# Weight combinations of a two-layer transformer kernel, made by adding transfers from GpSimd

## The chip, the cores and the metric

The kernel runs on one core of a Trainium2 chip. The metric is the device time of one execution in microseconds (us), the median of several runs. The core's engines are TensorE (PE; weight loads are shown apart as PEld), VectorE (DVE), ScalarE (ACT), GpSimd (POOL) and SyncE (SP). Each works through a queue of its own in order; they wait for each other through semaphores. Transfers (DMAs) are issued by one of the queues and carried by 16 DMA engines.

## The reference

Two layers, each an attention part and a feed-forward part, on x of 2048 tokens by 1024:

```python
def A(x):                                   # H = 32 heads of 32, W = 8 keys, dilation 2
    q, k, v = split(x @ wqkv)
    logits[s, w] = q[s] . k[s - 2 w] * 32 ** -0.5      # masked where s - 2 w < 0
    return concat_heads(softmax(logits) @ v[s - 2 w]) @ wo
def B(x):                                   # F = 3584
    return relu(x @ w1 + b1) ** 2 @ w2 + b2
x = x + A(layernorm(x));  x = x + B(layernorm(x))
x = x + A(layernorm(x));  x = x + B(layernorm(x))
```

All inputs are bfloat16; the kernel works in float16 and bfloat16 with float32 sums.

## The kernel before

**Units.** A layer's tokens are cut into four groups of 512 (four tiles of 128). With two layers there are eight units, u = 0 to 7, and each goes through the same stages: `SA` (load x, LayerNorm, transpose into `xnA`), `SQ` or `SQ7` (q, k, v), `S2` (attention), `SW` or `SW7` (product with wo, residual, second LayerNorm into `xnB`), `SF1` (FFN1: relu squared, into `r2`) and `SF2` (FFN2, residual, `out_tile`). Unit u+1's attention is worked on while unit u's FFN runs.

**Seven products.** The large matrix products use a Strassen scheme in Winograd's form: a 2 by 2 block product from seven products (`product`, L657, order and banks from `seven` and `AT`) into PSUM banks X, Y and Z. Three of the seven take raw blocks of the weights (`RAW`), four take combinations of blocks (`COMB`: products 5, 7, 6, 3). The moving side has combinations too (`T`, `TA`, made by `rhs_combos`, L682). ACT copies the first product's bank to seed another (`seed_first`, L590), and DVE and ACT put the results together.

**Where the combinations are made.** The weights' combinations are the same for all units. They are made once, in units 0 and 1, by DVE: four tensor_tensor operations (`tv`) for each block, each followed by a store of 256 KB into DRAM scratch (`sw` for w1, `sqv` for q and v, `sk` for k; `tw` and `two` for w2 and wo). `keep_w1` (L661) does this for the seven blocks of w1 (28 operations, L674), `keep_wqkv` (L513) for k (8) and for q and v (16). Later units load them back by `w<-sw` and so on, 1 MB each. Unit 0 itself computes q, k, v without the scheme (`SQ`, chunks `pq` on PE at L879, cast by ACT at L884), and so does unit 1; unit 0's FFN1 (`SF1_plain`, L1196) does its first `PLAIN1` = 1 block of seven without it (`ph`, L1222 and L1226) and the others from the tiles that DVE has just made.

**Attention.** In `S2` (L920) DVE multiplies q with the shifted k (`P`, L941), sums the products of chunks in a tree (L949) of a given depth, and PE sums over the rest and over a head's lanes (`lg`, L956; four matmuls for each leaf). `DEP0` is that depth for the two halves of unit 0's tokens; eight chunks at depth 1 leave four leaves, at depth 3 one. After the softmax (ACT, DVE) DVE does the weighted sum with v (`pr`, `o`: L1020, L1027).

**The start.** Unit 0's tiles 0 to 2 of x are normalised by `ln_first` (statistics and normalisation on DVE), tile 3 by `ln` with statistics and normalisation on ACT (L740 to L750). PE transposes them (`pt`, L800), DVE copies the transposes to `xnA` (L803). `XACT` = (1, 2) puts the loads of two tiles on ACT's queue, the other loads are on SP's. Unit 1's LayerNorms follow on ACT (L740 to L748, L719).

**What sets the order.** The stages only register operations with an engine, an estimated duration, buffers and a priority. The class `Plan` simulates the engines with these durations, picks by priority, and shifts priorities by the lists of seeds in `ORDER`. What comes out is one fixed queue for each engine. At run time nothing but these queues and the waits for data and buffers sets the order; the argument `after` of an operation holds in the plan alone.

Of the kernel before, what the change touches and what calls it, by code (L numbers as in the profile page):

```python
# [27 lines left out]
FOLD = (0, 1, 2)  # L28
# [9 lines left out]
XACT = (1, 2)  # L38
# [10 lines left out]
DEP0 = (1, 1)  # L49
NEARLY = 4  # L50
PLAIN1 = 1
# [3 lines left out]
RT = 4  # L55
PR1 = 20.0
XT = 2
# [67 lines left out]
class Plan:  # L125
# [45 lines left out]
    def schedule(self):  # L171
# [19 lines left out]
        def fits(o):  # L191
            if o.mb and len(landed) >= LANES and landed[-LANES] > t + 1e-9:
# [28 lines left out]
        landed = []  # L221
# [3 lines left out]
        while left:  # L225
            progress = False
            for e in engs:
# [13 lines left out]
                if o.mb:  # L241
                    dma_free = max(dma_free, end) + o.mb / DMA_MBS
                    end = dma_free
                    landed.append(end + o.lat)
# [84 lines left out]
class _Kernel:  # L329
    def __init__(self, ctx, tc, x, wqkv, wo, w1, b1, w2, b2, out, n_layers=2):  # L330
# [16 lines left out]
        self.state = {}  # L347

    def setup(self):
# [36 lines left out]
        todo = {"k": [("k", 0), ("k", 1)], "qv": [("q", 0), ("q", 1), ("v", 0), ("v", 1)], "w1": list(range(self.NDP))}  # L386
        self.orders = {j: interleave(d) for j, d in todo.items()}
# [12 lines left out]
        p.caps.update(pk=2, pj=2, lg=4, w=8, xt=XT, P0=4, P1=4, pr=2, pb=2, dn=1, e=1, xm=6, xnA=1, xnB=1, xn=3, xo=2, q=1, k=1, v=1, o=1, r2=1, s1=1, tv=4, T=1, TA=1, tr=3, wl=2, u=6, y=4, yq=4, yxm=2, yxa=2, yxo=2, ri=1, yw=4, so=1)  # L400
# [12 lines left out]
    def dma(self, out, src, r, w, mb, prio=None, after=(), name="dma", cast=None, lat=None, eng="SP", dur=None):  # L413
# [3 lines left out]
        return self.p.add(eng, dur or 0.08, fn, r, w, self.nxt() if prio is None else prio, after, mb=mb, name=name, lat=lat)  # L417

# [140 lines left out]

    def seven(self, job, xnT, T, make):  # L560
# [6 lines left out]
        for d, pr in order:  # L567
# [8 lines left out]
            else:  # L576
                if d not in ws:
                    w = ws[d] = Buf("8K", "w", [128, 4, 4, 256], F16)
                    key = (job,) + (d if isinstance(d, tuple) else (d,))
                    self.dma(lambda w=w: w[:], lambda d=d: self.scr[job][d][:], [(key, i) for i in range(4)], [(w, 0)], 4 * 0.256, name="w")  # L580
# [5 lines left out]
    def seven_banks(self):  # L586
        return [Buf("ps", nm, [128, 2, HB], F32, "seeded" if nm == "Y" else "") for nm in "XYZ"]

    def seed_first(self, X, Y):
        self.p.add("ACT", act(512), lambda: self.nc.scalar.copy(Y[:], X[:]), [(X, 0)], [(Y, 0)], UP, name="u")  # L590

    def qkv_step(self, u, nm, s):
# [13 lines left out]
        def keep(i):  # L606
            us[i] = Buf("1K", "u", [128, 2, HB], F16)
            p.add("ACT", act(512), lambda: nc.scalar.copy(us[i][:], X[:]), [(X, 0)], [(us[i], 0)], UP, name="u")  # L608

        def copy(bank):  # L610
            y = Buf("1K", "yq", [128, 2, HB], F16)
            p.add("ACT", act(512), lambda: nc.scalar.copy(y[:], bank[:]), [(bank, 0)], [(y, 0)], 1.5, name="yq")  # L612
# [9 lines left out]
        def mul(pr, w, wi, rhs, rc):  # L622
            bank, fm = self.product(pr, w, wi, rhs, X, Y, Z)
            self.state[u]["gate" + nm] = p.add("PE", 8 * MMH, fm, rc + [(w, 0)], [(bank, 0)], self.nxt(), name="fq")
            if pr == 1:
                self.seed_first(X, Y)
            elif pr == 5:
                us["y5"] = copy(Z)
# [32 lines left out]
    def keep_w1(self, dp, w):  # L661

        nc, p = self.nc, self.p

# [12 lines left out]
        comb(s3, lambda: raw(0, 0), lambda: raw(1, 0), ALU.subtract, [(w, 0), (w, 1)], 7)  # L677
        comb(s2, lambda: s1[:], lambda: raw(0, 0), ALU.subtract, [(w, 0), (s1, 0)], 6)
        comb(s4, lambda: raw(0, 1), lambda: s2[:], ALU.subtract, [(w, 0), (s2, 0)], 3)
        return {5: s1, 7: s3, 6: s2, 3: s4}  # L680

    def rhs_combos(self, xnT, prio, cls, tag, whole=False):  # L682
# [9 lines left out]
        def comb(i, a, b, ra, tl):  # L692
            p.add("DVE", dve(512), lambda: nc.vector.tensor_tensor(t(i)[:, tl], a()[:, tl], b()[:, tl], ALU.subtract),
                  ra, [(T, (i, tl))], prio, name="T")
        if whole:
            def both(i, a, b, ra):
                p.add("DVE", dve(1024), lambda: nc.vector.tensor_tensor(t(i), a(), b(), ALU.subtract), ra, [(T, (i, 0)), (T, (i, 1))], prio, name="T")
            lo, hi = [(xnT, 0), (xnT, 1)], [(xnT, 2), (xnT, 3)]
            both(0, lambda: B(0, 1), lambda: B(0, 0), lo + hi)
            both(1, lambda: B(1, 1), lambda: t(0), hi + [(T, (0, 0)), (T, (0, 1))])  # L700
            both(2, lambda: B(1, 1), lambda: B(0, 1), hi)
            both(3, lambda: B(1, 0), lambda: t(1), lo + [(T, (1, 0)), (T, (1, 1))])
            return T
        for tl in range(2):
            lo, hi = [(xnT, tl)], [(xnT, 2 + tl)]
            comb(0, lambda: B(0, 1), lambda: B(0, 0), lo + hi, tl)
            comb(1, lambda: B(1, 1), lambda: t(0), hi + [(T, (0, tl))], tl)
            comb(2, lambda: B(1, 1), lambda: B(0, 1), hi, tl)
# [3 lines left out]
    def ln(self, x, xv, xcells, xnT, tl, prio, vec, on_pe=False, tag="xn", after=(), vnorm=True, pv=-99.5, parts=1):  # L712
# [48 lines left out]
        if on_pe:  # L761
            return self.transpose(xn, xnT, tl, -10.0 if pv == -99.5 else pv, parts), xn
# [30 lines left out]
    def transpose(self, xn, xnT, tl, prio, parts=1):  # L793
# [3 lines left out]
        for i in range(parts):  # L797
# [4 lines left out]
            def f6(i=i):  # L802
                nc.vector.tensor_copy(xnT[:, tl, i * n:(i + 1) * n], pt[:, i * n:(i + 1) * n])  # L803
            p.add("PE", 0.65 / parts, f5, [(xn, 0)], [(pt, i)], prio, name="pt")
            op = p.add("DVE", 0.09 + 0.6 / parts, f6, [(pt, i)], [(xnT, tl if i == parts - 1 else (tl, i))], prio - 200.0, name="ptc")
# [12 lines left out]
    def SA(self, u):  # L818
# [7 lines left out]
        for tl in ORD if u == 0 else range(4):  # L826
# [3 lines left out]
            if u == 0 and tl == 3:  # L830
                self.ln(x, xv, [0], xnT, tl, -9e4, False, on_pe=True, tag="xn3", after=rst)
# [364 lines left out]
    def SF1_plain(self, u):  # L1196
# [50 lines left out]
        for i, (dp, pr) in enumerate(interleave(range(PLAIN1, self.NDP))):  # L1247
# [4 lines left out]
            if pr in s:  # L1252
                step(pr, s[pr], None, *rhs[pr])
            else:
# [17 lines left out]
    def ffn1_step(self, r2, dp, fold):  # L1272
# [7 lines left out]
        def keep(i):  # L1280
            us[i] = Buf("1K", "u", [128, 2, HB], F16)
            if not fold:
                p.add("ACT", act(512), lambda: nc.scalar.copy(us[i][:], X[:]), [(X, 0)], [(us[i], 0), (us[i], 1)], UP, name="u")
                return
            f = f0 + (h if i == 3 else 0)
            for a in range(2):
                p.add("ACT", 0.1 + act(256), lambda a=a: nc.scalar.activation(out=us[i][:, a, :], in_=X[:, a, :], func=ACTF.Identity,  # L1287
                                                                              bias=self.b1T[:, f + a:f + a + 1], scale=1.0),
                      [(X, 0)], [(us[i], a)], UP, name="u")

        def copy(bank):
            y = Buf("1K", "y", [128, 2, HB], F16)
            p.add("ACT", act(512), lambda: nc.scalar.copy(y[:], bank[:]), [(bank, 0)], [(y, 0)], 1.5, name="y")  # L1293
# [30 lines left out]
        def mul(pr, w, wi, rhs, rc):  # L1324
            bank, fm = self.product(pr, w, wi, rhs, X, Y, Z)
            self.ffs.append(p.add("PE", 8 * MMH, fm, rc + [(w, wi[0] if isinstance(wi, tuple) else 0)], [(bank, 0)], self.nxt(), name="ff"))
            if pr == 1:
                self.seed_first(X, Y)
            elif pr == 2:
                relu(Y, r1, f0)  # L1330
            elif pr == 5:
                us["y5"] = copy(Z)
# [104 lines left out]
    def out_tile(self, layer, t, db, py, xm, end=False):  # L1437
# [5 lines left out]
        if not end:  # L1443
            xo = Buf("1K", "xo", [128, BLK], BF)
            self.merge(py, lambda: xm[:, sl], lambda: xo[:], [(xm, db)], [(xo, 0)], "xo")
            self.dma(lambda: dst[:, sl], lambda: xo[:], [(xo, 0)], [(cell, db)], 0.14, prio=-10.0)
            return
        for i in range(2):
            xo = Buf("1K", "xo", [128, HB], BF)
            a, c = slice(i * HB, (i + 1) * HB), slice(db * BLK + i * HB, db * BLK + (i + 1) * HB)  # L1450
            p.add("DVE", dve(HB, False), lambda xo=xo, a=a, c=c: nc.vector.tensor_tensor(xo[:], py[:, a], xm[:, c], ALU.add),
                  [(py, i), (xm, db)], [(xo, 0)], -100.0, name="xo")
            self.dma(lambda c=c: dst[:, c], lambda xo=xo: xo[:], [(xo, 0)], [(cell, (db, i))], 0.07, prio=-10.0)
# [34 lines left out]
    def build(self):  # L1488
# [8 lines left out]
        self.run(self.SQ(0, "v"))  # L1497
        self.biases()
# [46 lines left out]
def _lay(name, a):  # L1545
# [7 lines left out]
    if name == "A_wqkv":  # L1553
        a = a.reshape(2, 4, 128, 3, 128, 4, 2).transpose(3, 5, 2, 0, 1, 6, 4).reshape(3, 4, 128, 2, 1024)
        get = lambda d, m, k: a["qkv".index(d[0]), 2 * m + d[1], :, k]
        a = np.concatenate([a.reshape(-1)] + raws(get, [("k", 0), ("k", 1)]) + raws(get, [("q", 0), ("q", 1), ("v", 0), ("v", 1)]))
    elif name == "A_wo":
        a = a.reshape(128, 8, 2, 512).transpose(2, 0, 1, 3).reshape(256, 4096)
    elif name == "B_w1":
        a = a.reshape(8, 128, 2, 7, 256).transpose(3, 1, 2, 0, 4).reshape(7, 128, 2, 2, 1024)  # L1560
        a = np.concatenate([a.reshape(-1)] + raws(lambda d, m, k: a[d, :, m, k], range(7)))
# [27 lines left out]
```

## Time and profile before

| what | us |
|---|---|
| median of 3 runs (1133.49, 1133.62, 1139.12) | 1133.62 |
| profiled execution | 1134.86 |
| its span | 1133.1 |
| busy in the span: PE, DVE, ACT, POOL | 1122.6, 996.4, 800.2, 1.8 |
| first matmul of q and k (pq) starts at | 9.96 |
| last matmul ends at | 1129.74 |

The span is from the first to the last instruction of the profiled execution; 1.76 us lie outside of it. Busy times of engines overlap. In the rows of a profile, "128x512 f16" is partitions by elements and type, "xN" the number of instructions, and "<-" in brackets names what ended the idle time ahead of an instruction. The granted TensorE clock is 1.00 in all of the profile.

### The profile page before, as it was taken

The numbers are of one execution on the slowest core, as the hardware profiler recorded it, in microseconds if no ns is written. First come the engines' busy times: TensorE is split into PE (matmuls) and PEld (weight loads), VectorE is DVE, ScalarE is ACT, GpSimd is POOL, SyncE is SP. The second block draws the span as 40 slices with busy tenths as digits, with TensorE's granted clock in tenths as the row PEclk, the third lists the DMA queues.
The fourth block names the chain that finished last, engine by engine and source line by source line (L and its number), as shares of the span: only waits on it lengthen the run. The fifth ranks groups of instructions, "written<-read, shape, count | busy, mean of one in ns | idle before, by whom it ended". The sixth has DMA issues, their size and how long they took to land.

```text
span 1133.1 us, 20734 instructions
## 1 busy us (share of the span) xinstructions
PE 1122.6 (99%) x7872; PEld 771.8 (68%) x7919; DVE 996.4 (88%) x1541; ACT 800.2 (71%) x1602; POOL 1.8 (0%) x8
## 2 busy tenths in 40 slices
PE   8999999999999999999999999999999999999998
PEld 6645764678846787468864688557884678845864
DVE  7999999999997999959999699997999789997341
ACT  6733897467985789757993669856797478933861
POOL 0000000000000000000000000000000000000000
PEclk9999999999999999999999999999999999999999
DMA  9966789999999996999979997999979999689882
GB/s 368 289 207 242 233 265 322 324 350 366 379 348 365 350 387 251 337 357 362 369 264 359 381 335 278 333 313 416 347 268 331 374 378 377 215 314 311 333 301 93
DMA packets 141053, 362.34 MB, mean 320 GB/s; under 512 B 67866, under 2 KB 76186, under 8 KB 120602
## 3 DMA queue, kind: packets, MB, share of 16 engines
q1 hardware_dynamic: 140666, 360.50, 91.3%
q8 instruction: 62, 1.02, 0.4%
q10 hardware_dynamic: 288, 0.52, 0.1%
q14 instruction: 37, 0.30, 0.1%
HBM read 314.84 MB, written 31.46 MB: 306 GB/s over the span
## 4 chain that ended last, share of the span: by engine, by line
PE 90%; ACT 5%; DMA 3%; issue 1%; DVE 0%; DVEq 0%; SPq 0%; ACTq 0%
PE X L657 25%; PE X L1379 14%; PE Z L657 12%; PE Z L1379 7%; PE pq L879 7%; PE Y L657 6%; PE py L1075 4%; PE Y L1379 3%; PE py L479 3%; PE X L1146 3%; PE lg L956 1%; PE Z L1146 1%; ACT r L1314 1%; DMA w<-in_B_w_dram 1%; ACT u L1287 1%; ACT rr L1320 1%
## 5 line engine op out<-in xcount | busy, mean ns | idle before, releaser
L657 PEld LDWEIGHTS <-w 128*128 128x128 f16 (+1 forms) x4904 | 479.5, 98 | 72.2 <-DMA w<-in_B_w_dram 1.3
L1379 PEld LDWEIGHTS <-r 128*128 128x128 f16 x1183 | 115.7, 98 | 134.8 <-issue 0.2
L1379 PE MATMUL X<-w,r 128*128 128x512 f16 (+2 forms) x784 | 177.0, 377 | 0.4
L941 DVE TENSOR_TENSOR P<-q,k 128x2048 f16<-128x2048 f16 x128 | 153.9, 1225 | 1.9 <-ACT q L620 1.0
L657 PE MATMUL X<-T,w 128*128 128x256 f16 x1224 | 153.2, 273 | 0.0
L1020 DVE TENSOR_TENSOR pr<-pb,v 128x4096 f16<-128x4096 f16 x64 | 146.2, 2298 | 0.5 <-PE Y L657 0.3
L949 DVE TENSOR_TENSOR P<-P,P 128x2048 f16<-128x2048 f16 x106 | 129.2, 1222 | 0.2
L1314 ACT ACTIVATE r<-rr 128x1024 f16<-128x1024 f16 x110 | 123.9, 1140 | 0.5 <-DVE rr L1306 0.2
L1027 DVE TENSOR_TENSOR pr<-pr 128x1024 f16<-128x1024 f16 (+1 forms) x128 | 118.4, 955 | 0.0
L657 PE MATMUL X<-TA,w 128*128 128x256 f16 x864 | 108.6, 273 | 0.0
L590 ACT COPY Y<-X 128x512 f32<-128x512 f32 x115 | 70.6, 615 | 36.6 <-PE X L657 33.6
L879 PE MATMUL pq<-xnA,w 128*128 128x256 f16 (+1 forms) x512 | 86.5, 326 | 0.0
L1293 ACT CAST y<-Z 128x512 f16<-128x512 f32 x110 | 70.6, 655 | 6.0 <-PE Z L657 5.9
L879 PEld LDWEIGHTS <-w 128*128 128x128 bf16 x512 | 49.9, 98 | 32.1
L1297 DVE TENSOR_TENSOR rr<-u,y 128x512 f16<-128x512 f16 x110 | 46.2, 424 | 24.4 <-ACT y L1293 13.1
L1320 ACT ACTIVATE rr<-Y,b1T 128x256 f16<-128x256 f32 x110 | 54.2, 538 | 4.4 <-PE Y L657 3.3
L657 PE MATMUL Y<-xnB,w 128*128 128x256 f16 x440 | 56.7, 273 | 0.0
L657 PE MATMUL X<-xnB,w 128*128 128x256 f16 x440 | 55.9, 273 | 0.8 <-DMA w<-in_B_w_dram 0.8
L1320 ACT ACTIVATE rr<-X,b1T 128x256 f16<-128x256 f32 x110 | 55.7, 563 | 0.6 <-PE X L657 0.6
L612 ACT CAST yq<-Z 128x512 f16<-128x512 f32 x72 | 41.9, 586 | 18.5 <-PE Z L657 18.0
L608 ACT CAST u<-X 128x512 f16<-128x512 f32 x72 | 42.0, 586 | 18.2 <-PE X L657 17.5
L657 PE MATMUL Z<-xnB,w 128*128 128x256 f16 x392 | 50.8, 273 | 0.1
(159 smaller groups left out, 1648.8 us busy)
## 6 DMA issues: line engine op xcount, KB each, us to landing
w<-sw SPq DMA_DIRECT2D x49, 1024.0 KB, 10.3
w<-tw SPq DMA_DIRECT2D x56, 896.0 KB, 6.8
w<-in_B_w_dram SPq DMA_DIRECT2D x42, 896.0 KB, 5.8
w<-in_B_w_dram SPq DMA_DIRECT2D x35, 1024.0 KB, 10.9
w<-in_A_wqkv_dram SPq DMA_DIRECT2D x32, 1024.0 KB, 10.9
w<-sqv SPq DMA_DIRECT2D x24, 1024.0 KB, 11.2
w<-in_B_w_dram SPq DMA_DIRECT2D x28, 512.0 KB, 6.2
w<-sk SPq DMA_DIRECT2D x12, 1024.0 KB, 8.7
```

Of the source, the lines that this page charges most:

```text
L590: self.p.add("ACT", act(512), lambda: self.nc.scalar.copy(Y[:], X[:]), [(X, 0)], [(Y, 0)], UP, name="u")
L657: nc.tensor.matmul(bank[:, a, :], lw[:, k, a * 128:(a + 1) * 128], rhs(k), start=(start and k == 0 and a == 0), stop=(k == 3), skip_group_ ...
L879: nc.tensor.matmul(pq[:, t0 * HB:t1 * HB], w[:, c0 // 2 % 2, kd // 4, kd % 4, c0 % 2 * 128:c0 % 2 * 128 + 128], xnT[:, 2 * t0:2 * t1, kd, ...
L941: nc.vector.tensor_tensor(cur[:], q[:, c, None, hb * HB:(hb + 1) * HB].to_broadcast([128, W, HB]), _win_ap(k[:, c, :], HALO + hb * HB, HB) ...
L949: nc.vector.tensor_tensor(other[:], other[:], cur[:], ALU.add)
L1020: p.add("DVE", dve(4096), lambda pr=pr, ch=ch: nc.vector.tensor_tensor(pr[:], pb[:].unsqueeze(1).to_broadcast([128, 2, W, HB]), _win_ap2(v ...
L1027: nc.vector.tensor_tensor(dst, pr[:, :, 0:n, :], pr[:, :, n:2 * n, :], ALU.add)
L1293: p.add("ACT", act(512), lambda: nc.scalar.copy(y[:], bank[:]), [(bank, 0)], [(y, 0)], 1.5, name="y")
L1297: p.add("DVE", dve(512), lambda: nc.vector.tensor_tensor(r[:, :, m, :], us[i][:], y[:], ALU.add), [(us[i], 0), (us[i], 1), (y, 0)], [(r, ( ...
L1314: p.add("ACT", 0.955, lambda: nc.scalar.activation(out=r2[:, f:f + 2, :].rearrange("p a t -> p (a t)"), in_=r[:].rearrange("p a m t -> p ( ...
L1320: p.add("ACT", 0.36, lambda a=a: nc.scalar.activation(out=r[:, a, 0, :], in_=bank[:, a, :], func=ACTF.Relu, bias=self.b1T[:, f + a:f + a + ...
L1379: nc.tensor.matmul(banks[q][:, lo:hi], left(jj, q), w[:, j, lo:hi], start=(start and jj == 0), stop=(jj == h - 1), skip_group_check=True)
```

## The change

- **Combinations in DRAM.** For w1, q and v, `make` issues 44 transfers from GpSimd's queue: for each of eleven blocks (seven of w1, two each of q and v) a copy of 1 MB from DRAM to DRAM, bfloat16 to float16, and then transfers of 512, 256 and 256 KB that add to what lies there, each waiting for the one before it on that block. The host lays out copies of the weights' blocks for it (`SUM`). DVE's operations and stores for w1, q and v are gone; k's stay. `make` asks the planner to put the transfers after the last load of a weight for v.
- **All as sums.** An adding transfer can't subtract, so the combinations are sums, and the signs move to the combinations of the moving side, to ACT's copies (now activations of Identity with scale 1 or −1) and to the seed: product 1 goes to bank Y, and `seed_minus` writes X = −Y.
- **FFN1 of unit 0.** `PLAIN1` goes from 1 to 3; the other four blocks load their combinations from `sw` (1 MB each on SP's queue).
- **Logit tree of unit 0.** `DEP0` goes from (1, 1) to (3, 3).
- **The start.** Tiles 2 and 3 of unit 0 are normalised on ACT (`LNA`), and ACT copies their transposes (`CPT`). All four loads of x are on SP's queue.
- **Output.** `out_tile` writes the sum in place in `xm`, and rows are stored as tiles of 256 KB, not 128 KB each half (the last four tiles as before).
- **Order.** New seeds.

The matmuls on PE go from 2440 to 2480 of 128x512 and from 5414 to 5302 of 128x256; `tv` operations from 88 to 44; transfers on SP's queue from 600 to 534, on GpSimd's from 0 to 44.

```diff
-XACT = (1, 2)
+XACT = ()
...
-DEP0 = (1, 1)
+DEP0 = (3,3)
...
-PLAIN1 = 1
+PLAIN1 = 3
...
+SUM = ((1, 0), (0, 0), (0, 0), (0, 1), (1, 1), (1, 0))
+DM = ("w1", "qv")
+MKS = ("w1", "qv")
+LNA = (2, 3)
+CPT = ("xn3",)
...
+    def make(self, blocks, after=()):
+
+        p = self.p
+
+        def steps(job, d):
+            n = self.todo[job].index(d) + (2 if job == "qv" else 0)
+            src = (self.w1 if job == "w1" else self.wqkv)[self.at[job == "w1"] + n * 128 * 6144:][:128 * 6144].rearrange("(p n) -> p n", n=6144)
+            key = (job,) + (d if isinstance(d, tuple) else (d,))
+            dst = lambda a, b: self.scr[job][d][:, a:b].rearrange("p i k n -> p (i k n)")
+
+            def step(a, b, src, r, mb, op=None):
+                def fn():
+                    self.nc.gpsimd.dma_start(dst(a, b), src(), **({} if op is None else {"accum_op": op}))
+                return lambda: p.add("POOL", POOL_ISSUE, fn, r, [(key, i) for i in range(a, b)], self.nxt(), after, mb=mb, name="mk", lat=POOL_LAT)
+            return [step(0, 4, lambda: src[:, 0:4096], (), MK_COPY), step(0, 2, lambda: src[:, 4096:6144], (), 2 * MK_ADD, ALU.add),
+                    step(2, 3, lambda: dst(0, 1), [(key, 0)], MK_ADD, ALU.add), step(3, 4, lambda: dst(2, 3), [(key, 2)], MK_ADD, ALU.add)]
+
+        for i in range(0, len(blocks), 2):
+            for pair in zip(*[steps(*b) for b in blocks[i:i + 2]]):
+                for add in pair:
+                    add()
 
...
     def keep_wqkv(self, nm, ws, after=()):
...
+        if job in DM:
+            return
...
-            comb(s3, lambda: raw(0, 0), lambda: raw(1, 0), ALU.subtract, [w0, w1], 7)
-            comb(s2, lambda: s1[:], lambda: raw(0, 0), ALU.subtract, [w0, (s1, 0)], 6)
-            comb(s4, lambda: raw(0, 1), lambda: s2[:], ALU.subtract, [w0, (s2, 0)], 3)
+            comb(s3, lambda: raw(0, 0), lambda: raw(1, 0), ALU.add, [w0, w1], 7)
+            comb(s2, lambda: s1[:], lambda: raw(0, 0), ALU.add, [w0, (s1, 0)], 6)
+            comb(s4, lambda: raw(0, 1), lambda: s2[:], ALU.add, [w0, (s2, 0)], 3)
...
+    def combos(self, job, d):
+        w = Buf("8K", "w", [128, 4, 4, 256], F16)
+        key = (job,) + (d if isinstance(d, tuple) else (d,))
+        self.dma(lambda: w[:], lambda: self.scr[job][d][:], [(key, i) for i in range(4)], [(w, 0)], 4 * 0.256, name="w")
+        return w
...
+    def seed_minus(self, X, Y):
+        self.p.add("ACT", act(512), lambda: self.nc.scalar.activation(out=X[:], in_=Y[:], func=ACTF.Identity, scale=-1.0), [(Y, 0)], [(X, 0)], UP, name="u")
...
-        bank = {1: X, 6: X, 7: X, 4: X, 2: Y, 5: Z, 3: Z}[pr]
+        bank = {1: Y, 6: X, 7: X, 4: X, 2: Y, 5: Z, 3: Z}[pr]
...
     def keep_w1(self, dp, w):
+        if "w1" in DM:
+            return self.combos("w1", dp) if dp >= PLAIN1 else None
...
-            both(0, lambda: B(0, 1), lambda: B(0, 0), lo + hi)
+            both(0, lambda: B(0, 0), lambda: B(0, 1), lo + hi)
+            both(1, lambda: B(1, 1), lambda: t(0), hi + [(T, (0, 0)), (T, (0, 1))], ALU.add)
...
+        (nc.scalar.copy if act else nc.vector.tensor_copy)(xnT[:, tl, i * n:(i + 1) * n], pt[:, i * n:(i + 1) * n])
...
-            if u == 0 and tl == 3:
+            if u == 0 and tl in LNA:
+                self.ln(x, xv, [0], xnT, tl, -9e4, False, on_pe=True, tag="xn3", after=rst, vnorm=tl == 3)
...
         self.run(self.SQ(0, "v"))
+        ld = [o for o in self.p.ops if o.name == "w"][-1:]
+        self.make([(job, d) for job in MKS for d in self.todo[job]], ld)
         self.biases()
         self.S2(0, DEP0)
```

More of the change, by code (lines that the diff above doesn't have):

```diff
@@ L243, in schedule @@
                     end = dma_free
-                    landed.append(end + o.lat)
+                    landed[o.eng == "POOL"].append(end + o.lat)
                 out.append((t, len(out), o))
@@ L347, in __init__ @@
         self.state = {}
+        self.half = set()
     def setup(self):
@@ L1282, in keep @@
             if not fold:
-                p.add("ACT", act(512), lambda: nc.scalar.copy(us[i][:], X[:]), [(X, 0)], [(us[i], 0), (us[i], 1)], UP, name="u")
+                p.add("ACT", act(512), lambda: nc.scalar.activation(out=us[i][:], in_=X[:], func=ACTF.Identity, scale=-1.0 if i == 2 else 1.0), [(X, 0)], [(us[i], 0), (us[i], 1)], UP, name="u")
                 return
@@ L1331, in mul @@
             elif pr == 5:
[L1332 removed]
+                us["y5"] = copy(Z, -1.0)
             elif pr == 6:
@@ L1442, in out_tile @@
         cell = ("out" if final else "xs", layer, t)
[L1443 to L1446, printed above, removed]
-            return
[L1448 to L1453, printed above, removed]
+        o = lambda: xm[:].bitcast(BF)
+        if end:
+            for i in range(2):
+                a, c = slice(i * HB, (i + 1) * HB), slice(db * BLK + i * HB, db * BLK + (i + 1) * HB)
+                p.add("DVE", dve(HB, False), lambda a=a, c=c: nc.vector.tensor_tensor(o()[:, c], py[:, a], xm[:, c], ALU.add),
+                      [(py, i), (xm, db)], [(xm, (db, i))], -100.0, name="xo")
+                self.dma(lambda c=c: dst[:, c], lambda c=c: o()[:, c], [(xm, (db, i))], [(cell, (db, i))], 0.07, prio=-10.0)
+            return
+        self.merge(py, lambda: xm[:, sl], lambda: o()[:, sl], [(xm, db)], [(xm, db)], "xo")
+        if final and t >= self.NT - 4:
+            self.dma(lambda: dst[:, sl], lambda: o()[:, sl], [(xm, db)], [(cell, db)], 0.14, prio=-10.0)
+        elif t in self.half:
+            self.dma(lambda: dst, lambda: o(), [(xm, 0), (xm, 1)], [(cell, 0), (cell, 1)], 0.27, prio=-10.0)
+            self.half.discard(t)
+        else:
+            self.half.add(t)
     def run(self, a, b=(), pace=1):
```

85 lines of the change are left out of this document (47 added, 38 removed), and 16 rows, old and new, of the table ORDER.

## The prediction

> **What bounds the kernel now.** I read the engine rows of the page first, then the chain that ended last, then the windows.
>
> ```profile
> span 1133.1 us, 20734 instructions
> PE 1122.6 (99%) x7872; PEld 771.8 (68%) x7919; DVE 996.4 (88%) x1541; ACT 800.2 (71%) x1602; POOL 1.8 (0%) x8
> ...
> PE 90%; ACT 5%; DMA 3%; issue 1%; DVE 0%; DVEq 0%; SPq 0%; ACTq 0%
> ```
>
> TensorE is busy 99% of the span, at clock 1.00 throughout, and is the chain. So an edit pays by what it takes off PE's matmuls, and costs by any wait that it gives PE. POOL does next to nothing. The windows show where waits are near (busy us of each engine, clock, DMA share, GB/s):
>
> ```profile
> 5.00:10.00 5.00, 3.01 (x26) 1.63 (x25) 4.78 (x13) 2.92 (x8) 0.00 (x0) 1.00 1.03 409
> 10.00:30.00 20.00, 20.00 (x185) 17.26 (x184) 18.44 (x24) 15.81 (x43) 0.00 (x0) 1.00 1.03 406
> 60.00:90.00 30.00, 29.95 (x140) 13.51 (x140) 30.00 (x36) 11.30 (x20) 0.00 (x0) 1.00 0.47 161
> 90.00:110.00 20.00, 19.95 (x125) 10.78 (x125) 20.00 (x36) 8.31 (x20) 0.00 (x0) 1.00 0.88 320
> 110.00:170.00 60.00, 59.95 (x453) 44.08 (x452) 59.93 (x95) 52.84 (x105) 0.00 (x0) 1.00 0.76 243
> ```
>
> From 5 to 30 us the DMA engines are full at 406 to 409 GB/s; from 60 to 110 us VectorE (DVE) has no idle time and PE just none either. The order there decides, so I read the timeline: ACT at the start, DVE and PE where unit 0's FFN begins.
>
> ```profile
> 7.91 1.04 ACT L740 ACTIVATE xn<-x 128x1024 f16<-128x1024 bf16 x1
> ...
> 9.31 1.15 ACT L744 ACTIVATE xn<-x,sm 128x1024 f16<-128x1024 bf16 x1
> ...
> 11.04 0.38 ACT L884 CAST k<-pq 128x256 f16<-128x256 f32 x1
> ```
> ```profile
> 13.19 1.23 DVE L941 TENSOR_TENSOR P<-q,k 128x2048 f16<-128x2048 f16 x1 [0.23 <-ACT q L884]
> ...
> 111.58 0.69 DVE L803 COPY xnB<-pt 128x1024 f16<-128x1024 f16 x1
> ```
> ```profile
> 103.38 1.89 PE L879 MATMUL pq<-xnA,w 128*128 128x512 f16 x8
> ...
> 107.29 1.03 PE L1226 MATMUL ph<-xnB,w 128*128 128x256 f16 x8
> ```
>
> One LayerNorm on ACT delays the first cast by 3.1 us (7.91 to 11.04). DVE's run from the first product of unit 0's attention (13.19) to the last copy of FFN1's input (111.58, done 112.2) is one unbroken queue. PE does unit 1's chunks (pq) while it waits for that input, and starts FFN1 of unit 0 (ph) at 107.29.
>
> **The change, part by part.** Spacings on PE are 0.2157 us for a 512-wide matmul and 0.1091 for a 256-wide. From the first pq at 9.96 us, PE's matmuls times these spacings give 1115.6 us; the last one ends at 1129.74, so only 4.2 us were lost underway, and the tail is 3.4.
>
> *PE's work.* A tree at full depth saves 24 lg matmuls: −24 × 0.2157 = −5.2. Two more plain blocks add 64 ph of 512 (+13.8) and remove 112 of 256 from the products (−12.2). Together −3.6 us. The new sign pattern adds no matmul; ACT's copies become activations of the same shape (0.48 to the next one either way).
>
> *DVE's work up to FFN1 of unit 0.* I counted both queues between the two DVE lines shown. Before: 20 products and 10 tree sums at 1.135 from start to start, 22 combinations tv at 0.60, the eight av groups and the rest: 97.1 us; 13.2 + 97.1 = 110.3, against 112.2 in the trace, so the count holds within 2. After: products 26 (+6.8), tree sums 22 (+13.6), tv 8 (k's) instead of 22 (−8.4), two xnA copies gone to ACT (−1.2): 107.9. So DVE does fewer combinations in all (44 of 88 gone, some 26 us over the whole run), yet before FFN1 it has 10.8 us more: deeper trees, and unit 1's products moved ahead.
>
> *ACT at the start.* Tile 2's LayerNorm joins tile 3's on ACT, ahead of the first cast: 1.17 + 0.23 + 1.28 + 0.45 = 3.1 us, so the first cast goes to about 13.9. Up to the q cast that DVE's eighth product waits for, the queue then holds 16 casts (0.26), two LayerNorms of unit 1 (4.6 each: 1.17 + 0.23 + 1.28 + 0.8 + 1.14), one normalise (1.14), two small ones (0.5), and two copies of transposes, new on ACT (1.05 each, an estimate from the 128x512 cast's 0.585 and the 128x1024 activation's 1.14): 17.1, so it ends at 31. DVE's own queue would be there at 23.5 (13.2 + 10.3). DVE is 7.5 us late, and has no slack to 112. PE, whose banks wait for the same casts, loses about 4.6 by 29 us and 3.6 more at 60 to 64, inside what follows.
>
> *Where it lands.* 13.2 + 107.9 + 7.5 = 128.6 for the last xnB copy; ph can start about 1.2 earlier, 127.4. PE's own sum reaches that point at 113.85, because in the new order all 24 chunks of unit 1 stand ahead of it; before, 8 of them (13.8 us) were left to fill in. So PE waits 13.6 us in all. If that cover had stayed, this would cost nothing.
>
> *Inside FFN1 of unit 0*, without chunks between the products, ACT must free a bank for each product; it was busy 52.8 of 60 us at 110 to 170. Bounds 0 (it keeps up, as later) and 7 (the 88% over the 60 us that FFN1 takes, if it runs short by as much as it had idle). I take 3, nearer to the later units, where PE lost 4 us in 1000.
>
> *GpSimd's 44 transfers.* Eleven blocks, each a 1 MB copy from DRAM to DRAM and then adds of 512, 256 and 256 KB that wait for one another. No operation of this kind is in the trace. The first copies wait for no data (the "after" of the planner makes no wait), so 2 MB and the next steps fall into 5 to 30 us, where the engines are full. 1 MB at 410 GB/s is 2.44 us; between 0 MB and 4.2 MB land there. x of unit 1 has 2.5 us of slack before ACT needs it, the first weights have none: 0 to 9 us, I take 5, by the full share 1.03. The Trainium skill, DMA: Bandwidth & Descriptors, section Issuing engines are not separate DMA queues, says that GpSimd's transfers run on the same 16 engines and interleave; with half of 20 full microseconds it would be 10 here, and the sum 1157.
>
> *The chain of adds* after that: by the rows of before,
>
> ```profile
> w<-sw SPq DMA_DIRECT2D x49, 1024.0 KB, 10.3
> ...
> w<-in_B_w_dram SPq DMA_DIRECT2D x28, 512.0 KB, 6.2
> ...
> sqv<-tv SPq DMA_DIRECT2D x16, 256.0 KB, 5.6
> ```
>
> a pair of blocks takes 10.3 + 6.2 + 2 × 5.6 = 27.7 us, two at a time: the block that SP loads first (dp3) is ready at 55, dp6 at 103. SP gets to that load at about 100 us; PE wants the blocks from 149 to 165, plus its delay. Hidden, so 0, with a bound in the rival. The same four loads add 4 MB, in a window at share 0.76: 0. x loads all on SP: w is issued 0.85 us later, inside the 5 above. Stores of whole tiles from xm: off the path.
>
> *Sum.* 1134.9 (profiled execution) − 3.6 + 13.6 + 3 + 5 = 1152.9; the median of before lies 1.2 below its profiled run, so **1152 us**.
>
> **Rivals.**
>
> *GpSimd's chain holds SP's queue* (slower still). SP's load of dp3 waits for four adds, and raw weights of dp4, unit 2's x and its transposes are queued behind it. With every step f times as long, dp3 is ready at 55f and dp6 at 103f, landing 10.3 later, against about 183 for PE in the delayed schedule. It decides from f = 1.7; at f = 2 PE waits 33 us more (1185), at 2.5 it would be 85. For: an add must also read what it adds to, and DVE fills its time. Against: the rows used include queueing at a full share. The Trainium skill, SBUF — State Buffer, the warning on the "DVE blocks DMA" trap in the section SBUF: two separate sides, says that GpSimd cannot write descriptors while DVE holds the shared port; no row of before shows such a transfer.
>
> *The waits do not reach PE* (no change). If casts and LayerNorms on ACT overlap better than start to start, and DVE catches up as its tv work has gone, only −3.6 remains with part of the contention: 1128 to 1139, about 1131. For: DVE has 26 us less overall. Against: these 26 come mostly after FFN1 begins.
>
> *All waits vanish, the old ones too* (faster): −3.6 and up to the old 4.2: 1126. For: the old losses lie at 163 to 262 us, where DVE was full. Against: it needs chunks that no longer stand there to fill.
>
> *The change does not do what it says:* the transfers are meant for idle time (share 0.47 at 60 to 90) but start at launch. If all 4.2 MB get in ahead of first weights, 9 instead of 5, and 1156; this is in my own range.
>
> **How the numbers follow.** My case (1140 to 1163: contention 0 to 9, ACT 0 to 7) 0.60; the chain late (1163 to 1200) 0.21; waits not at PE (1128 to 1139) 0.12; all gone (below 1128) 0.07. Predicted 1152. The range of 1136 to 1184 leaves out the last case, some 0.07 of the third and 0.06 above. Half a per cent, 5.7 us, is about what a measurement of this kernel tells from no change: faster (below 1127.9) 0.07, same 0.12, slower (above 1139.3) 0.81.
>
> **What would show it.** Right: first cast on ACT near 14, DVE idle before a product near 24 to 31 with an ACT q cast as releaser; last xnB copy near 128; PE idle before ph and pt, released by DVE, together about 13 us from 20 to 130. After that PE's matmuls end 1008 + 3 to 7 us later. DMA share over 1 before 30 us with bytes on a POOL queue. Wrong: no PE idle before ph (the DVE count), waits on w<-sw with SP idle on POOL transfers (the chain), or first pq after 15 (contention heavier).

## The result, and the profile after

The changed kernel takes 1214.13 us (median of 3 runs, 1212.89 to 1214.22) against 1133.62: ratio 1.0697, interval 1.0676 to 1.0718. The forecast was 1152 with a range up to 1184. Slower was right; the size was not.

The page of the changed kernel: engine rows, the clock granted to TensorE in 40 slices, the queues of the transfers (packets, MB, time as a share of 16 engines over the span), and the chain:

```profile
span 1211.2 us, 20389 instructions
PE 1131.8 (93%) x7800; PEld 769.1 (63%) x7847; DVE 973.1 (80%) x1489; ACT 804.1 (66%) x1601; POOL 34.8 (3%) x52
...
PEclk7795899999999999999999999999999999999999
...
q1 hardware_dynamic: 131162, 353.68, 84.5%
q0 software_dynamic: 6336, 23.07, 8.1%
...
PE 61%; ACT 15%; DVE 6%; DMA 2%; issue 1%; DVEq 0%; ACTq 0%
```

TensorE fell from 99% to 93% of a longer span, and its chain from 90% to 61%. All low digits of the clock lie in the first sixth. q0 is GpSimd's queue: 23 MB, and 8.1% of 1211.2 us, that is as much as 98 us of all 16 engines. The windows of the changed kernel over the same stretches (busy us by engine, clock, DMA share, GB/s):

```profile
5.00:10.00 5.00, 3.76 (x27) 1.74 (x25) 3.81 (x10) 0.99 (x4) 0.00 (x0) 1.00 1.03 388
10.00:30.00 20.00, 10.47 (x55) 7.47 (x56) 0.55 (x1) 9.74 (x24) 4.09 (x5) 0.66 1.05 323
60.00:90.00 30.00, 27.84 (x185) 17.93 (x183) 24.94 (x28) 20.09 (x47) 5.08 (x8) 1.00 1.12 270
90.00:110.00 20.00, 2.07 (x9) 0.99 (x7) 19.91 (x19) 2.74 (x6) 3.96 (x6) 0.52 1.11 263
110.00:170.00 60.00, 44.72 (x199) 20.07 (x202) 29.50 (x33) 16.45 (x30) 12.01 (x17) 0.85 1.04 270
```

The DMA share is over 1 from 5 to 170 us, also where it was 0.47 to 0.88 before (a share over 1 means that packet times on an engine overlap and are counted twice). From 10 us on fewer bytes move at that share: 263 to 323 GB/s instead of 406. TensorE does next to nothing from 90 to 110 us. Its waits over the whole trace (us in total, times, longest) name what it lacked:

```profile
PE pq L923 <- issue: 31.3, 1, 31.3
PE pk L1527 <- DMA b1r<-in_B_b_dram: 12.7, 1, 12.7
PE pq L923 <- DMA w<-in_A_wqkv_dram: 10.4, 2, 6.2
```

The 31.3 us have no releaser in that view. The timeline shows the chunk that stood still (PE) and what SyncE was at meanwhile:

```profile
125.18 24.15 PE L923 MATMUL pq<-xnA,w 128*128 128x512 f16 x104 [31.32 <-issue]
```
```profile
85.69 29.71 SPq L809 DMA_TRANSPOSE xnA<-xn  x1
```

The chunk reads unit 1's transposes xnA. One transpose held SyncE's queue for 29.7 us; the longest of xnA before was 5.2. The longest time from issue to landing of a transpose in this trace is 39.4 us, and 85.7 + 39.4 is 125.1, when the chunk starts. A load of 7 KB (b1r) was late enough to cost 12.7. The steps at the start and at FFN1 of unit 0, in the timelines of ACT, DVE and PE:

```profile
14.12 1.06 ACT L783 ACTIVATE xn<-x 128x1024 f16<-128x1024 bf16 x1 [7.14 <-DMA x<-in_A_x_dram]
...
19.69 0.36 ACT L928 CAST k<-pq 128x256 f16<-128x256 f32 x1
```
```profile
186.84 1.88 DVE L847 COPY xnB<-pt 128x1024 f16<-128x1024 f16 x3
```
```profile
187.67 1.03 PE L1270 MATMUL ph<-xnB,w 128*128 128x256 f16 x8 [1.20 <-DVE xnB L847]
```

ACT's LayerNorm waited for x, the first cast came at 19.7 (forecast 14), and FFN1 of unit 0 at 187.7 (forecast 127.4): the 60 us between forecast and result are all there by then.

### The profile page after: what moved, and what is told of

Its sections match the earlier page's. It is cut to its first block, busy times and chain, and to the rows that moved or that the text cites. A ratio compares the mean times of both kernels' runs of the same rounds, so it can differ in the third digit from the quotient of the medians.

```text
span 1211.2 us, 20389 instructions
## 1 busy us (share of the span) xinstructions
PE 1131.8 (93%) x7800; PEld 769.1 (63%) x7847; DVE 973.1 (80%) x1489; ACT 804.1 (66%) x1601; POOL 34.8 (3%) x52
## 4 chain that ended last, share of the span: by engine, by line
PE 61%; ACT 15%; DVE 6%; DMA 2%; issue 1%; DVEq 0%; ACTq 0%
PE X L698 13%; PE Z L698 9%; PE Y L698 9%; PE X L1428 9%; PE Z L1428 5%; PE py L510 4%; ACT r L1363 4%; PE X L1190 3%; ACT rr L1369 3%; PE py L1119 2%; PE Y L1428 2%; ACT y L1342 2%; PE Z L1190 1%; DVE pr L1064 1%; PE ph L1266 1%
## 5 line engine op out<-in xcount | busy, mean ns | idle before, releaser
L698 PEld LDWEIGHTS <-w 128*128 128x128 f16 (+1 forms) x4984 | 487.5, 98 | 77.0 <-issue 6.4
L698 PE MATMUL X<-T,w 128*128 128x256 f16 x1272 | 160.1, 273 | 1.9 <-ACT u L1336 1.8
L923 PE MATMUL pq<-xnA,w 128*128 128x256 f16 (+1 forms) x512 | 94.0, 349 | 44.2 <-issue 31.3
L698 PE MATMUL Y<-xnB,w 128*128 128x256 f16 x848 | 107.5, 273 | 1.0 <-ACT X L630 1.0
L698 PE MATMUL Y<-xnA,w 128*128 128x256 f16 x576 | 72.7, 273 | 0.0
L1342 ACT ACTIVATE y<-Z 128x512 f16<-128x512 f32 x106 | 67.8, 647 | 5.2 <-PE Z L698 4.7
L630 ACT ACTIVATE X<-Y 128x512 f32<-128x512 f32 x89 | 54.5, 613 | 20.1 <-PE Y L698 19.8
L648 ACT ACTIVATE u<-X 128x512 f16<-128x512 f32 x72 | 42.5, 598 | 22.1 <-PE X L698 21.8
L698 PE MATMUL Z<-T,w 128*128 128x256 f16 x424 | 55.0, 273 | 1.4 <-DMA w<-sw 1.4
L653 ACT ACTIVATE yq<-Z 128x512 f16<-128x512 f32 x72 | 42.5, 597 | 16.9 <-PE Z L698 16.3
## 6 DMA issues: line engine op xcount, KB each, us to landing
w<-in_A_wqkv_dram SPq DMA_DIRECT2D x32, 1024.0 KB, 10.6
w<-sqv SPq DMA_DIRECT2D x24, 1024.0 KB, 10.6
```

Of the source, the lines that this page charges most:

```text
L630: self.p.add("ACT", act(512), lambda: self.nc.scalar.activation(out=X[:], in_=Y[:], func=ACTF.Identity, scale=-1.0), [(Y, 0)], [(X, 0)], U ...
L698: nc.tensor.matmul(bank[:, a, :], lw[:, k, a * 128:(a + 1) * 128], rhs(k), start=(start and k == 0 and a == 0), stop=(k == 3), skip_group_ ...
L923: nc.tensor.matmul(pq[:, t0 * HB:t1 * HB], w[:, c0 // 2 % 2, kd // 4, kd % 4, c0 % 2 * 128:c0 % 2 * 128 + 128], xnT[:, 2 * t0:2 * t1, kd, ...
L1342: p.add("ACT", act(512), lambda: nc.scalar.activation(out=y[:], in_=bank[:], func=ACTF.Identity, scale=by), [(bank, 0)], [(y, 0)], 1.5, na ...
```

## The experiments

Theory T, formed on this trace: GpSimd's transfers take the DMA engines from SyncE's loads, transposes and small loads. Rival R: the new order of the queues itself loses the time, with the transfers as bystanders. The edits below are shortened.

**The transfers taken out of the changed kernel.** The edit leaves the order of all queues as it is; the loads that read from the input no longer wait for adds.

```diff
-                    self.nc.gpsimd.dma_start(dst(a, b), src(), ...)
+                    pass
 def combos(self, job, d):
-        self.dma(lambda: w[:], lambda: self.scr[job][d][:], ...)
+        self.dma(lambda: w[:], <the first 4096 columns of d's block in the input>, ...)
```

> The changed kernel with its queues as they are, but none of the 44 transfers of GpSimd is issued; the loads of combinations of w1, q and v take the same number of bytes straight from the weights' input instead, so that part of the result is left out. Theory T (the transfers take the DMA engines from SyncE's loads, transposes and small loads in the first 190 us): what is left is the order of the queues alone, which the prediction priced without contention at 1133.6 - 3.6 + 13.6 + 3 = 1147; 1143 to 1151, first matmul of q and k near 10 us, FFN1 of unit 0 near 127 us. Rival R (the loss of 80 us lies in the new order of the queues itself, above all SyncE's transposes for unit 1 ahead of the loads): still over 1170, with waits for xnA of 20 us and more.

Measured: 1154.33, ratio 1.0171 (1.0142 to 1.0200); span 1152.7. So the order costs 19.6 us of the span and the transfers 58.5 (1211.2 − 1152.7). T holds for the larger part; the order is 7 us dearer than its forecast and lies 3 us above T's range. Its timelines on DVE and PE:

```profile
18.20 1.23 DVE L991 TENSOR_TENSOR P<-q,k 128x2048 f16<-128x2048 f16 x1 [1.53 <-ACT q L934]
...
30.79 3.51 DVE L991 TENSOR_TENSOR P<-q,k 128x2048 f16<-128x2048 f16 x3 [0.65 <-ACT q L934]
```
```profile
130.22 1.03 PE L1276 MATMUL ph<-xnB,w 128*128 128x256 f16 x8 [1.20 <-DVE xnB L853]
```

DVE waits for ACT's q cast until 30.8 (forecast 31, though for the eighth product; here it is the fifth), and FFN1 starts at 130.2 (forecast 127.4).

**The transfers added to the kernel before**, whose order is untouched. Three kernels: from the launch on, behind the first attention output, and in small pieces.

```diff
+    # once, ahead of the first operation (late: behind a read of unit 0's o on the same queue)
+    for each pair of the eleven blocks, d a spare tile in DRAM, s a part of w1:
+        gpsimd.dma_start(d[:, 0:4096], s[:, 0:4096])
+        gpsimd.dma_start(d[:, 0:2048], s[:, 4096:6144], accum_op=add)
+        gpsimd.dma_start(d[:, 2048:3072], d[:, 0:1024], accum_op=add)
+        gpsimd.dma_start(d[:, 3072:4096], d[:, 2048:3072], accum_op=add)
+    # small pieces: the same rows as 256 elements out of every 512
```

> The kernel before with its order, plus 44 transfers of the same kinds, sizes and chaining on GpSimd's queue from the launch on, from w1's input into DRAM that nobody reads. Theory T: the kernel before loses most of what the changed one lost, 45 to 70 us, so 1180 to 1205, with the first matmul of q and k 4 to 6 us late and transposes of unit 1 that take 15 us and more to land. Rival R: its order gives the loads enough lead; below 1150.

Measured: 1200.15, ratio 1.0579 (1.0538 to 1.0619). The transfers alone cost a good order 65 us; the longest transpose for unit 1 holds SyncE's queue for 20.4 us, and FFN1 of unit 0 starts at 163.7 instead of 107.3, so most of the loss lies ahead of it. T again, though the first matmul of q and k came at 10.66, only 0.7 us late where 4 to 6 were expected.

> As the one with transfers from the launch on, but GpSimd first waits for the first finished part of unit 0's attention output (about 66 us), so that the transfers fall into the stretch from 66 to some 180 us, where the kernel before uses the DMA engines at shares of 0.47 to 0.88. Theory T, the start alone is hurt because SyncE's queue is full there: 1134 to 1145. Rival (any overlap with loads or transposes hurts, wherever it lies): over 1155, with waits for w or xnA between 90 and 180 us.

Measured: 1207.32, ratio 1.0642 (1.0605 to 1.0679). The start alone is not what is dear; my expectation failed. GpSimd's chain begins at 63 us and issues its last transfer at 281, far past 170, where the engines are full anyway. No transpose held SyncE's queue for more than 6.2 us here; the longest wait of PE, ACT and DVE was ACT's, 23.3 us for a load of x. So a held transpose is one form of the loss and not its condition.

> As the one with transfers from the launch on, with the same bytes in pieces of 512 bytes (rows of 8, 4 and 2 KB before). Theory P (the queues take turns packet by packet, so that a small packet of SyncE's transposes waits for one large packet of GpSimd's): with small packets the transposes of unit 1 land in under 9 us again and the time falls by 20 us or more against the same traffic in large pieces. Rival E (what counts is the engines' time for the bytes): no better than with large pieces, or worse, since small pieces take more time for each byte.

Measured: 1201.82, ratio 1.0594 (1.0551 to 1.0637). Transposes do move better (longest hold 10.6 us instead of 20.4, longest landing 18.4 instead of 31.3), but GpSimd's queue now takes 13.2% of the span, 159 us of the engines instead of 102, and the run is no shorter. Rival E's forecast came true. Theory P's did not, neither for the landing (under 9 us) nor for the time; turn-taking by packets does not explain the loss.

**What is dear in them.** Copies alone, four blocks alone, adds alone, and spread over the run, each on the kernel before (the same edit with fewer lines, with 4 blocks, with two copies and then adds only, with one or two blocks behind each unit's attention output).

> The kernel before plus only the eleven copies of 1 MB on GpSimd's queue from the launch on, without the adds. Theory C (capacity: with all 44 transfers GpSimd's queue took 8.5% of 1196.8 us = 102 us of all 16 engines, 65 of which were lost, so 37 were idle): the copies alone, if they move at the loads' rate of 410 GB/s, take 28 us and fit: 1134 to 1142, and the adds are the dear part, 73 us for as many bytes. If copies take as long per byte as adds (51 us), some 14 are lost: 1148. Rival S (what hurts is that GpSimd gets in first at the launch): 15 us and more in spite of fewer bytes, with the first matmul of q and k late.

> The kernel before plus the transfers of four blocks only (16 instead of 44) from the launch on. Theory C: 37 us of engine time against 37 us idle in the first 250, so the loss is small, 1134 to 1146, far under the 24 us that a loss in proportion to the bytes would give. Rival S: the start pays in full, 1155 and more.

> The kernel before plus two copies and then only the adding transfers of the eleven blocks (33 adds, 11.5 MB) from the launch on, all into the same two tiles of DRAM. The copies alone took 2.6% of 1161.8 us = 30 us of the engines for 11.5 MB and cost 29; all 44 transfers took 102. Theory C (an add takes the engines about 2.4 times as long per byte as a copy, and the loss follows the engines' time): GpSimd's queue shows 6 to 6.8% of the span, 72 to 80 us, and the run is 40 to 60 us longer than before, 1175 to 1195. Rival B (bytes decide): 13.6 MB like the copies' 11.5, 34 us longer at most, under 1170.

> The kernel before plus the same 44 transfers, but one or two blocks for each unit, each group waiting for that unit's attention output, so that they spread over the whole run. Theory C: the kernel before keeps the engines busy 92% of 1133 us, 90 us are idle in all, and the transfers need 102, so a part is lost even so: 1142 to 1165, far less than the 65 to 72 when bunched in the first 200 us. Rival (any transfer of GpSimd costs what it takes, wherever it lies): 1190 and more. Rival S (only the start is dear): under 1138.

GpSimd's queue in the page of each, in this order: copies, four blocks, adds:

```profile
q0 software_dynamic: 1584, 11.54, 2.6%
```
```profile
q0 software_dynamic: 2304, 8.39, 3.1%
```
```profile
q0 software_dynamic: 5040, 13.63, 6.2%
```

| kernel | engines' time for GpSimd (share of span) | longer span than its base |
|---|---|---|
| copies only | 2.6% of 1161.8 = 30 | 28.7 |
| four blocks | 3.1% of 1171.2 = 36 | 38.1 |
| adds (and two copies) | 6.2% of 1187.8 = 74 | 54.7 |
| all, from the launch | 8.5% of 1196.8 = 102 | 63.7 |
| all, late | 8.8% of 1205.3 = 106 | 72.2 |
| all, spread | 8.5% of 1198.0 = 102 | 64.9 |
| all, small pieces | 13.2% of 1202.2 = 159 | 69.1 |
| the changed kernel, against itself without | 8.1% of 1211.2 = 98 | 58.5 |

Medians and ratios: copies 1165.19 (1.0265, 1.0236 to 1.0295), four blocks 1172.73 (1.0332, 1.0309 to 1.0354), adds 1188.67 (1.0470, 1.0446 to 1.0493), spread 1194.39 (1.0523, 1.0455 to 1.0591). The engines' times and spans are of one profiled execution each; the spread kernel's lies 5 us above its median. Copies move at nearly the loads' rate, 2.6 us per MB (2.4 at 410 GB/s). Adds take the rest, 102 − 30 = 72 us for 11.5 MB, 6.2 us per MB; the run with adds gives 5.9 (74 less 5.5 for two copies). The Trainium skill, Collectives: The Full Stack, section The bandwidth ceiling: the fold count and why AG ≠ RS ≠ AR, says of the reducing step of a ring between cores that its add reads two sources and runs at about half a copy's rate; here an add takes 2.3 times as long. What makes it longer, no run here shows.

Of the four expectations of theory C only the one on the adds came true. That copies (1134 to 1142) and four blocks (1134 to 1146) would fit was wrong, as rival S had it: up to 36 us of such time from the launch are lost one for one. Of the larger amounts 0.60 to 0.74 is lost, and of the time for small pieces 0.43. That spreading helps was wrong too (1194.39, in the range of the rival): from 200 to 1100 us the kernel before has a DMA share of 0.89 to 1.03. With small pieces the share reaches 1.25 (60 to 90 us), so a part of their 159 us is counted twice; how much stays open. In the spread run, the first block, alone at 64 to 90 us, left no trace (TensorE busy 97.4 of the first 100 us, 96.8 before).

**One block, twice.** The same four transfers in the idle stretch and at the launch:

> The kernel before plus one block's four transfers (2.1 MB, some 9 us of the engines) that wait for unit 0's first attention output, at about 64 us, where the DMA share is 0.47 for the next 25 us. Theory C: no loss, 1132 to 1137 beside 1134 to 1136 without. Rival (every transfer costs its engine time): 1142 to 1146.

> The kernel before plus the same block's four transfers from the launch on, where the engines are full until 60 us. Theory C: 9 us lost, 1142 to 1147. Rival (a single block finds room): under 1138.

Measured: 1134.78, ratio 0.9998 (0.9985 to 1.0011), and 1142.12, ratio 1.0058 (1.0041 to 1.0074). Windows of the one in the idle stretch, then of the one at the launch:

```profile
0.00:30.00 30.00, 26.76 (x215) 20.07 (x216) 24.55 (x42) 19.87 (x51) 1.75 (x8) 1.00 0.96 368
...
60.00:90.00 30.00, 29.95 (x140) 13.48 (x140) 30.00 (x36) 11.27 (x20) 3.79 (x5) 1.00 0.79 230
```
```profile
0.00:30.00 30.00, 23.75 (x165) 15.96 (x166) 19.98 (x37) 13.87 (x38) 4.99 (x12) 0.96 0.97 343
```

In the idle stretch the share goes from 0.47 to 0.79 and TensorE loses nothing. At the launch the share stays at 0.97, TensorE loses 3 us of work in 30, FFN1 of unit 0 starts 6.8 us later than before (114.06 against 107.29), and the span grows by 7.8 for 8 us of the engines (0.7% of 1140.9). For one block this decides between the two theories: the price is engine time that is not idle at that moment. For the kernel before, all 44 transfers in large pieces fit roughly (102 and 106 us less some 30 idle in the first 200, against 64 and 72 lost); the small pieces do not. The Trainium skill, DMA: Bandwidth & Descriptors, section Issuing engines are not separate DMA queues, says that transfers of all issuing engines run on the same 16 DMA engines and interleave; the trace agrees, since the share in the idle stretch rises with GpSimd's transfers from 0.47 to 0.79.

**The same price in the changed order.** Transfers for the four blocks of w1 that unit 0 reads back:

```diff
+                    if d in (3, 4, 5, 6):
                         self.nc.gpsimd.dma_start(dst(a, b), src(), ...)
```

> The changed kernel with GpSimd's transfers only for the four blocks of w1 that unit 0 itself reads back (16 of 44); the other combinations are read straight from the weights' input, so that part is left out. Without any transfers this order took 1154 us, with all 44 1214, 60 more. Theory C (the loss follows the engines' time that is not idle; the same four blocks cost the kernel before 38 us for 36 us of engine time): 1180 to 1192. Rival L (the loss comes from the long chain of all eleven blocks, up to 190 us): under 1165.

Measured: 1189.88, ratio 1.0475 (1.0436 to 1.0513); 36.1 us of span over the kernel without, for 3.0% of 1188.8 = 36 us. That is in the range of theory C, and rival L is out. But C's reason does not give this size: the four blocks' last add is issued at 88 us, and without transfers this order leaves the engines 22 us idle in the first 95 (share 0.77). By that reason 14 us would be lost, and 36 were. Why the idle time was of no use there stays open.

**The order's share.** Six tree sums of unit 0 left out of the changed kernel without transfers:

```diff
-    p.add("DVE", dve(2048), fa, ..., name="tree")
+    p.add("DVE", dve(2048), fa if u or not lvl else (lambda: None), ..., name="tree")
```

> The changed kernel without GpSimd's transfers, as before, and without the six tree sums above the first level in unit 0's attention (that part of the sums is left out), all else as it is. Theory D (VectorE's queue sets the start of unit 0's FFN1): it starts 6.8 us earlier than the 130.2 us with all sums, near 123.5, and the whole run is 5 to 7 us shorter than the 1154 us, 1147 to 1149. Rival (PE's own losses at the start, waits for banks and a lower granted clock, set it): the start moves by under 3 us and the time stays above 1151.

Measured: 1153.94, ratio 1.0171 (1.0152 to 1.0189). FFN1 of unit 0 starts at 126.39, 3.8 us earlier, between the two forecasts, so DVE sets part of that start; TensorE no longer waits right before it, and its own losses ahead of it take the rest of the 6.8. The whole run did not get shorter, as the rival had it: by 332 us the lead is down to 1.6. TensorE now waits 2.2 us for loads of w between 268 and 297 (0.6 with all sums), where the share is 1.05.

Three kernels whose list of operations differs (the changed one without transfers and with the old start; the kernel before with the deep tree for both halves, and for one):

```diff
-LNA = (2, 3)    CPT = ("xn3",)    XACT = ()
+LNA = (3,)      CPT = ()          XACT = (1, 2)
```
```diff
-DEP0 = (1, 1)
+DEP0 = (3, 3)        # the third: (1, 3)
```

> The changed kernel without GpSimd's transfers (combinations read straight from the weights' input, so that part is left out), and with the start of the kernel before: tile 2 normalised on VectorE, transposes copied by VectorE, two tiles of x on ACT's queue. The planner makes a new order from this with the same seeds. Theory A (ACT's longer queue at the start makes VectorE 7.5 us late, and VectorE sets the start of unit 0's FFN1): first product on VectorE near 13, FFN1 of unit 0 5 to 8 us earlier than 130.2 us. Since six sums fewer moved that start by 4 us but the whole run by 0, the run gains less: 1146 to 1153. Rival (the start does not matter): FFN1 of unit 0 at 128 or later, 1153 to 1156.

> The kernel before with the logit tree of unit 0 at full depth as the only change: 24 matmuls less on TensorE (-5.2 us), 6 sums of 1.135 us more on VectorE before unit 0's FFN1. Theory D (VectorE's queue up to there has no slack, though eight chunks of unit 1 are left to fill TensorE's wait): between -5.2 and +1.6, so 1129 to 1136. Rival (the fill is used up and the wait returns in full): 1138 and more.

> The kernel before with the tree at full depth for the second half of unit 0's tokens alone: 12 matmuls less (-2.6 us), 3 sums more on VectorE (+3.4 us there). Theory D: the fill covers 3.4 us, so -2.6 to 0: 1131 to 1134, at the edge of what can be told from no change. Rival: VectorE's delay comes through, 1135 and more.

Measured: 1178.93 (1.0382, 1.0364 to 1.0399), 1187.25 (1.0457, 1.0442 to 1.0471), 1191.58 (1.0496, 1.0477 to 1.0515). None tells its two theories apart. In the first, FFN1 of unit 0 starts at 126.88, 3.3 us earlier than with the new start, again between the two forecasts. In the second it starts at 105.66, earlier than the 107.29 before. In both the time is lost all along after it: from 275 to 740 us TensorE is busy 450 and 451 of 465 us, 464 in the kernel before. The seeds in ORDER were given for another list of operations; with them the planner's order is some 25 us worse in the first (against the changed kernel without transfers) and 52 to 56 in the others. That the seeds are the reason is argued and not tested. What the old start or the deep tree is worth under an order of their own stays open. No kernel here is faster than the one before.

## Why the prediction was wrong, point by point

- **TensorE as the bound, and its work (−3.6).** The counts stand (7800 operations on PE against 7872). Without transfers the span is longer by −3.6 + 16.3 (FFN1 at 130.2 against 113.9 by the sum) + 9.6 lost after it on TensorE (forecast 3 to 7) − 4.2 that were lost before too + 1.5 of a longer tail after the last matmul = 19.6, as measured.
- **ACT at the start.** Right, seen without transfers: first cast 13.4 (forecast 13.9; its own terms, 11.04 + 3.1, give 14.1), the product on DVE that waits for ACT's q cast 30.8 (31).
- **DVE's count.** Right in size without transfers: last xnB copy done at 131.3 (128.6), FFN1 at 130.2 (127.4). The sign given for it, TensorE idle for DVE for about 13 us, is not there: of its waits up to 130 us, 4.7 name DVE, 4.0 ACT and 1.5 loads. The rest of the 16.3, about 6 by difference, goes with a lower granted clock (0.94 up to 60 us, 0.50 from 65 to 70), for which the sum had no term. That DVE would decide in the changed kernel was wrong: there FFN1 came 57 us later through the transfers.
- **Inside FFN1 of unit 0 (3, bounds 0 to 7).** Right: TensorE waits 2.9 us for ACT between 171 and 180. Not forecast were 2.5 more up to 340 us.
- **GpSimd's transfers (5, bounds 0 to 9): the step that failed.** They cost 58.5. The prediction priced only what falls into the first 25 us, at 2.44 us per MB, and took the stretch behind it as cover. Three errors sit in it. An add takes 5.9 to 6.2 us per MB, not 2.44. The sum over all 44 transfers, about 100 us of all engines, was never made, though the profile of before gives what there is to cover it: over the first 100 us the share was 0.86, over the second 0.83, then 0.9 and more, so some 30 us in 200. And a share of 0.76 or 0.88 was read as room for all of it.
- **The chain of adds (hidden).** Right: SyncE issued the first load of dp3 at 159.7, long after its last add was issued at 69.9, and TensorE waited 1.4 us for sw in all. TensorE's longest wait, 31.3 us, was for a transpose and not for the result of these adds. So the rival that held SyncE by this chain was wrong as a mechanism; its prices, 1185 and 1237, lie on either side of the result by chance.
- **The other rivals.** The first copy is issued at 1.30 us, so the transfers do start at launch, and the first matmul of q and k comes at 15.3 instead of 10.0, which the prediction named as a sign of heavier contention. But the transfers cost 72 us also when they began at 63, so starting at launch is not what makes them dear. That the waits do not reach PE is out, since the order without transfers is 19.6 us slower.
- **The range.** Its top came from that rival alone. With about 100 us of engine time (at the adds' measured rate) against 30 idle, the bound for the transfers had to be 70, not 9.

## What to carry to other kernels

Work moved from an engine to transfers costs the DMA engines' time: add up bytes by rate over all of it, and set it against the engines' idle time in that stretch (1 − share, times its length), not against bytes in the first moments. That is an estimate and no more: in the kernel before it gives 72 us for all transfers from the launch on, where 64 were lost, and in the changed order 14 for four blocks, where 36 were lost. This kernel, whose DMA share is 0.9 on average, had room for the adds of one block in its one idle stretch, and not for four or eleven. All transfers here came from GpSimd; whether the same bytes cost the same from another queue was not tried. And a schedule fitted by seeds to one list of operations did not serve to judge a change of that list.

## What the runs showed of the hardware

- An adding transfer from DRAM to DRAM takes 5.9 to 6.2 us of all 16 engines per MB; a copy from DRAM to DRAM with a change of type takes 2.6, little more than a load (2.4 at 410 GB/s). One block alone in the idle stretch, 2.1 MB of both kinds beside a share of 0.79, took 10 us (0.9% of 1132.9).
- Beside rows of 8, 4 and 2 KB from GpSimd from the launch on, one transpose held SyncE's queue for 20.4 us in the kernel before and 29.7 in the changed one (6.9 at most in either without transfers); beside pieces of 512 bytes it was 10.6. With the transfers from 63 us on it was 6.2 at most. A load of 7 KB was 12.7 us late for TensorE. That the queues take turns by packets is not shown.
- The clock granted to TensorE fell to 0.66 (10 to 30 us) and 0.52 (90 to 110 us) in the changed kernel, where it was busy for 10.47 and 2.07 of 20 us; without transfers it was 0.91 and 1.00 there. The Trainium skill, TensorE: Matmul & The Clock Gate, section Part 1: The HAM clock gate (the "warmup" mystery), says that an idle TensorE is clocked at half rate until it has been busy for about 3.4 us; the trace agrees: the clock is 0.50 from 94 to 125 us, where TensorE stands still, 0.67 from 125 to 130, where it starts again, and 1.00 from 130 to 140. So the lower clock follows the waits here.
